# A fused sliding-window attention and SwiGLU kernel: a shorter VectorE chain for one token group, and attention sinks on four row groups of TensorE

## The chip, the cores and the metric

The kernel runs on one core of a Trainium2 chip. The metric is the device time of one execution in microseconds (us). Runs of one kernel mostly agree within 0.3%, but this kernel's runs differ by about 0.6 us with the clock that TensorE was granted; each run records its mean clock, and I compare like with like where it matters. A run more than 1.5% above the fastest of its kernel is marked slow and left out of the ratios (eight runs of run 15 below, one of run 8).

In the profile lines, PE is TensorE's matmuls, PEld its weight loads, DVE VectorE, ACT ScalarE and POOL GpSimd. PSUM is the memory that matmuls write; the kernel holds eight banks of it. A *row group* is 32 of the 128 rows of TensorE's array: `32*128` in a line is a matmul on one of them. *Half clock* is a stretch in which the granted clock reads 0.50.

Ratios below are the mean time of one kernel's fast runs over the mean time of the fast runs of the kernel before in the same rounds, so they are not quite the ratio of the medians that stand beside them. Brackets hold 95% intervals.

## The reference

Four batches, 8 heads, 768 positions, head size 64. Each query sees the last 128 keys and the first four (the *sinks*). The result, 3072 tokens of 512 numbers, goes through a gated feed-forward block.

```python
scores = scale * np.matmul(q, k.transpose(0, 1, 3, 2))
keep = (pos[None, :] < 4) | ((rel >= 0) & (rel < 128))   # rel = query position - key position
a = softmax(np.where(keep, scores, -1e9))
x = np.matmul(a, v)            # then [tokens, heads * 64]
g = x @ w_gate
return (g * sigmoid(g) * (x @ w_val)) @ w_out
```

## The kernel before

The 3072 tokens are cut in 12 attention *groups* of 256 tokens, three for each batch, and in eight feed-forward *token blocks* (three of 256, four of 512, one of 256). A unit of feed-forward work is a gate matmul set `pg`, a value set `pv`, and an element-wise pair `u`, `ht` on VectorE. A `weave` puts attention steps between the `pg` and the `pv` of a unit: transposes `T`, scores `S`, sink scores `K`, value products `PV`, output transposes `X`. Groups that are not the first of their batch have sinks: there `PV` starts with a full-row matmul of the sink probabilities `es` with a block-diagonal tile `vsb` of sink values.

```python
def step_K(g):                             # sink scores
    ps = bank([P, 256], FP32, "pk")
    for p in range(NP2):                   # 4 pairs of heads, 32 PSUM rows each
        nc.tensor.matmul(ps[32 * p:32 * p + KW], kss[:, b, p], qTs[b][:, p, c * 256:(c + 1) * 256], ...)
    es_t[g] = espool.tile([P, 256], BF16, tag="es", name="es")
    nc.scalar.activation(es_t[g], ps, AF.Exp, scale=scale)

def step_PV(g, j, hh):                     # 128 tokens x 4 heads
    po = bank([P, 4, D + 1], FP32, "o")
    mms = []
    if c > 0:
        mms.append((po, es_t[g][:, j * P:(j + 1) * P], vsbs[b][:, 4 * hh:4 * hh + 4]))
    ...                                    # then the window's 8 matmuls
    def dve():
        nc.vector.reciprocal(rcp, po[:, :, D:D + 1])
        nc.vector.tensor_tensor(xns[g, j]..., po[:, :, 0:D], rcp.broadcast_to([P, 4, D]), op=ALU.mult)
    later.append(dve)

def step_X(g, j, evict="v"):               # normalised rows xn -> xT, the input of the block
    if g >= XB:                            # XB = 4: groups 4 to 11 by DMA transpose
        nc.sync.dma_start_transpose(xTs[tb][:, :, off:off + P], xns[g, j])   # (queued)
    else: ...                              # TensorE transposes px, then a copy to xT

# prologue (cut): group 0
st = [rowp.tile([P, H, 2 * D], FP32, tag="rows", name="st") for _ in range(2)]   # k and q, 512-byte rows
...
pair_S(1); pair_T(3)
nc.vector.tensor_scalar(lt8, th8, float(NS), None, op0=ALU.is_lt)
nc.vector.scalar_tensor_tensor(diag_h, th8, 0.0, lt8, op0=ALU.is_ge, op1=ALU.mult)
pair_mask(0); pair_S(2); step_ks(0); pair_mask(1); ...

# groups 1 and 2
us = [g0[0], (alone, 0, 0), g0[1], (alone, 0, 0), g0[2], g1[0], ...]   # alone: a unit without gates
weave(us, slots((1, PVs(1)[:2]), (3, PVs(1)[2:]),
    (4, [A(step_X, 1, 0, "a"), A(step_X, 1, 1, "a")]), ...))

def pair(ga, gb, sh=0):                    # two groups in one 512-token block
    return [((s, s + 2), Ss(ga)), (s + 2, [K(ga)]), ((s + 4, s + 5, s + 6, s + 7), PVs(ga)),
            ((s + 6, s + 8), Ss(gb)), ((s + 8, s + 9), Xs(ga)), (s + 8, [K(gb)]), ...]
```

The softmax here doesn't subtract the row's maximum and nothing guards it: scores larger than these inputs give would overflow.

## Time and profile before

| | kernel before |
|---|---|
| median time | 248.36 us (248.31 to 248.96, 4 runs) |
| span of the profiled run | 246.7 us, TensorE busy 95% |
| first gate matmul (end of the prologue) | 15.60 us |
| first down-projection matmul `pd` | 64.06 us |
| first gate matmul of token block 3 | 83.84 us |
| from there to the end | 162.86 us |

The last four rows are starts of TensorE groups in the timeline. They cut the run in stretches with different limits: the prologue; groups 1 to 4 and blocks 0 to 2; the long steady part. A change is read by how it moves each milestone, not by shares of busy time. Each kernel has one profile, so a milestone has scatter: three kernels with the changed prologue, word for word, reach the first gate matmul at 20.95, 20.81 and 19.99 us (the changed kernel, runs 3 and 7). The prediction shows the lines for group 1 and for the sinks. Two more views of this trace matter later. The first is VectorE in the prologue (start, length, instruction, in brackets the idle time ahead of it and what ended it):

```profile
8.72 0.41 DVE L497 CAST qT<-pt 128x256 bf16<-128x256 f32 x1
9.06 0.16 DVE L531 TENSOR_SCALAR lt<-th 128x8 f32<-128x8 f32 x1
9.25 0.17 DVE L532 SCALAR_TENSOR_TENSOR diag_h<-th,lt 128x8 bf16<-128x8 f32 x1
9.33 0.55 DVE L516 TENSOR_TENSOR e<-e,mask 128x768 bf16<-128x768 bf16 x1
...
10.18 1.50 DVE L516 TENSOR_TENSOR e<-e,mask 128x768 bf16<-128x768 bf16 x3
```

The four masks follow the last cast at once, and nothing waits for a load. The second is the DMA rate in the first 14 us, in 40 slices of 0.35 us:

```profile
GB/s 0 0 0 0 0 95 110 59 285 350 341 344 347 350 341 338 221 195 192 194 189 191 198 178 164 157 153 158 164 190 187 197 192 199 196 196 167 168 155 156
```

From the tenth slice (3.15 us) the input loads run on a plateau near 345 GB/s.

### The profile page before, as it was taken

The numbers are of one execution on the slowest core, as the hardware profiler recorded it, in microseconds if no ns is written. First come the engines' busy times: TensorE is split into PE (matmuls) and PEld (weight loads), VectorE is DVE, ScalarE is ACT, GpSimd is POOL, SyncE is SP. The second block draws the span as 40 slices with busy tenths as digits, with TensorE's granted clock in tenths as the row PEclk, the third lists the DMA queues.
The fourth block names the chain that finished last, engine by engine and source line by source line (L and its number), as shares of the span: only waits on it lengthen the run. The fifth ranks groups of instructions, "written<-read, shape, count | busy, mean of one in ns | idle before, by whom it ended". The sixth has DMA issues, their size and how long they took to land.

```text
span 246.7 us, 5043 instructions
## 1 busy us (share of the span) xinstructions
PE 235.0 (95%) x1981; PEld 136.5 (55%) x2004; DVE 163.7 (66%) x345; ACT 111.7 (45%) x219; POOL 67.8 (27%) x89
## 2 busy tenths in 40 slices
PE   7796999999999999999999999999999999999994
PEld 3485787787645445444445454445454445478443
DVE  5988378876955199992298993198980389887100
ACT  4893347234654473621564721555611662333112
POOL 8955735984680007250053000000000000000000
PEclk9999799999999999999999999999999999999999
DMA  7999999999999449994479302551103200100132
GB/s 187 183 185 196 191 206 195 156 159 141 156 178 216 144 106 89 128 139 110 128 127 156 51 3 85 148 129 25 43 3 120 92 0 3 43 3 0 43 128 85
DMA packets 100390, 27.61 MB, mean 112 GB/s; under 512 B 85392, under 2 KB 97424, under 8 KB 100368
## 3 DMA queue, kind: packets, MB, share of 16 engines
q0 software_dynamic: 68384, 13.64, 67.4%
q1 hardware_dynamic: 30928, 13.15, 22.9%
q10 hardware_dynamic: 1056, 0.52, 0.7%
q8 instruction: 15, 0.25, 0.4%
q14 instruction: 7, 0.06, 0.1%
HBM read 28.34 MB, written 6.29 MB: 140 GB/s over the span
## 4 chain that ended last, share of the span: by engine, by line
PE 84%; DVE 9%; ACT 4%; issue 1%; DVEq 0%
PE pd L416 25%; PE pv L385 24%; PE pg L385 22%; PE o L329 4%; PE s L283 3%; ACT e L290 3%; DVE ht L399 3%; PE pt L235 2%; DVE xn L335 2%; DVE u L398 1%; PE w L473 1%; DVE e L516 1%; PE pt L489 1%; DVE e L295 1%; ACT th L392 0%
## 5 line engine op out<-in xcount | busy, mean ns | idle before, releaser
L385 PE MATMUL pv<-xT,wv 128*128 128x256 bf16 (+1 forms) x374 | 74.7, 328 | 1.5 <-DVE ht L399 0.9
L392 ACT ACTIVATE th<-pg 128x512 f32<-128x512 f32 x72 | 43.5, 605 | 71.3 <-PE pg L385 69.3
L385 PE MATMUL pg<-xT,wg 128*128 128x256 bf16 (+1 forms) x380 | 74.8, 328 | 0.2
L398 DVE SCALAR_TENSOR_TENSOR u<-th,pg 128x512 bf16<-128x512 f32 x72 | 49.2, 683 | 34.4 <-ACT th L392 34.1
L416 PE MATMUL pd<-wo,ht 128*128 128x512 bf16 (+1 forms) x291 | 65.0, 370 | 0.6 <-issue 0.2
L399 DVE TENSOR_TENSOR ht<-u,pv 128x512 bf16<-128x512 bf16 x72 | 49.5, 688 | 11.9 <-PE pv L385 5.4
L385 PEld LDWEIGHTS <-wg 128*128 128x128 bf16 x384 | 37.8, 99 | 25.5 <-issue 0.2
L385 PEld LDWEIGHTS <-wv 128*128 128x128 bf16 x384 | 34.7, 99 | 21.2 <-issue 2.8
L290 ACT ACTIVATE e<-s 128x512 bf16<-128x512 f32 (+1 forms) x88 | 42.9, 583 | 3.1 <-PE s L283 3.0
L416 PEld LDWEIGHTS <-ht 128*128 128x128 bf16 x300 | 28.0, 98 | 28.6 <-issue 0.3
L420 ACT ACTIVATE ot<-pd 128x512 f32<-128x512 f32 (+1 forms) x25 | 14.6, 583 | 50.9 <-PE pd L416 50.9
L295 DVE TENSOR_TENSOR e<-e,mask 128x1024 bf16<-128x1024 bf16 (+1 forms) x44 | 27.0, 649 | 3.3 <-ACT e L290 3.2
L110 POOL DMA_DIRECT2D nat<-in_k_dram x16 | 14.2, 901 | 46.5 <-DMA qT<-nat 42.4
L121 POOL DMA_DIRECT2D va<-in_v_dram x24 | 21.5, 912 | 5.4 <-DMA nat<-in_q_dram 2.6
L335 DVE TENSOR_TENSOR xn<-o,rcp 128x256 bf16<-128x256 f32 x48 | 20.4, 424 | 1.7
L329 PEld LDWEIGHTS <-e 128*128 128x128 bf16 x352 | 16.8, 98 | 7.1 <-DVE e L516 1.0
L329 PE MATMUL o<-va,e 128*128 128x65 bf16 x352 | 18.4, 193 | 0.7 <-DVE e L516 0.7
L110 POOL DMA_DIRECT2D nat<-in_q_dram x16 | 14.3, 909 | 1.8 <-DMA nat<-in_k_dram 1.6
L334 DVE RECIPROCAL rcp<-o 128x4 f32<-128x4 f32 x48 | 8.5, 177 | 7.4 <-PE o L329 7.2
L283 PE MATMUL s<-qT,kT 64*128 64x128 bf16 (+1 forms) x240 | 12.9, 237 | 0.0
L283 PEld LDWEIGHTS <-kT 64*128 64x128 bf16 x240 | 7.7, 94 | 6.9 <-issue 6.4
L329 PE MATMUL o<-vsb,es 128*128 128x260 bf16 x32 | 8.8, 274 | 0.3 <-ACT es L309 0.3
(56 smaller groups left out, 89.9 us busy)
## 6 DMA issues: line engine op xcount, KB each, us to landing
out_dram<-ot SPq DMA_DIRECT2D x23, 256.0 KB
va<-in_v_dram POOLq DMA_DIRECT2D x24, 128.0 KB, 7.5
nat<-in_k_dram POOLq DMA_DIRECT2D x16, 128.0 KB, 6.7
nat<-in_q_dram POOLq DMA_DIRECT2D x16, 128.0 KB, 7.3
wo<-in_moe_w_out_dram POOLq DMA_DIRECT2D x4, 384.0 KB, 12.3
wg<-in_moe_w_gate_dram POOLq DMA_DIRECT2D x4, 256.0 KB, 8.4
wv<-in_moe_w_val_dram POOLq DMA_DIRECT2D x4, 256.0 KB, 8.9
rows<-in_k_dram POOLq DMA_DIRECT2D x6, 128.0 KB, 9.0
```

Of the source, the lines that this page charges most:

```text
L110: nc.gpsimd.dma_start(x[:, i, j].rearrange("p (h d) -> p h d", d=D), src[b, :, t0:t0 + P].rearrange("h p d -> p h d"))
L121: nc.gpsimd.dma_start(va[:, j, :, 0:D], v[b, :, t0:t0 + P].rearrange("h p d -> p h d"))
L283: nc.tensor.matmul(pss[2 * pp + h][:, col:col + n], kTs[b][r, p, kk:kk + P], qTs[b][r, p, qq:qq + n], start=True, stop=True)
L290: nc.scalar.activation(e_t[g][:, h0 + h, lo:512], pss[2 * pp + h][:, lo:512], AF.Exp, scale=scale)
L295: nc.vector.tensor_tensor(e, e, m[:, :, lo:512].broadcast_to([P, 2, 512 - lo]), op=ALU.mult)
L329: nc.tensor.matmul(o, l, r, start=(i == 0), stop=(i == len(mms) - 1), skip_group_check=True)
L335: nc.vector.tensor_tensor(xns[g, j][:, 256 * hh:256 * (hh + 1)].rearrange("p (h d) -> p h d", h=4), po[:, :, 0:D], rcp.broadcast_to([P, 4, ...
L385: nc.tensor.matmul(ps[:, i * n:(i + 1) * n], ws[fi][:, c, fo * P:(fo + 1) * P], x[:, c], start=(c == 0), stop=(c == DMC - 1))
L392: nc.scalar.activation(th, pg, AF.Tanh, scale=0.5)
L398: nc.vector.scalar_tensor_tensor(u, th, 1.0, pg, op0=ALU.add, op1=ALU.mult)
L399: nc.vector.tensor_tensor(hts[tb][:, f:f + two].rearrange("p a n -> p (a n)"), u, pv, op=ALU.mult)
L416: nc.tensor.matmul(po, hts[tb][:, f, ts * P:(ts + 1) * P], wos[f // n][:, f % n, lo:hi], start=(f == 0), stop=(f == DFC - 1))
```

## The change

The intent is fourfold. Half of group 1's division goes from VectorE to ScalarE, and the two units without gates go away. The sinks of a group become four matmuls of 32 rows each, on four row groups of TensorE, into four PSUM banks that are opened together. The sink scores move to the first scores of a group. Group 2's outputs come later and are evicted by ScalarE. For the new rows, the sink values `vcf` are needed twice, so 64 partitions of them are copied to the other 64.

```diff
-    diag_h = const.tile([P, H], BF16)
+    diag_h = const.tile([P, 4], BF16)
-    th8 = const.tile([P, H], FP32)          # lt8 the same
+    th8 = const.tile([P, 4, 4], FP32)
-            nc.sync.dma_start(vcf[32 * p + NS * w:..., :, 0:D], ...)
+        r = 32 * (h // 4) + NS * (h % 4)
+        nc.sync.dma_start(vcf[r:r + NS, :, 0:D], ...)
@@ step_ks, step_vsb
-            nc.vector.tensor_copy(kss ...)   # 2 in all
+            nc.vector.tensor_copy(kss ...)   # 4 in all
-        vsb = const.tile([P, H, D + 1], BF16, tag=f"vsb{b}", name="vsb")
+        vsb = const.tile([P, 4, D + 1], BF16, tag=f"vsb{b}", name="vsb")
@@ step_K: 4 matmuls of 256 columns become 8 of 128, two accumulating on each 32 rows of PSUM
@@ new
+    def step_sinks(g):
+        for j in range(2):
+            for hh in range(2):
+                r = slice(32 * (2 * j + hh), 32 * (2 * j + hh + 1))
+                pos[j, hh] = bank([P, 4, D + 1], FP32, "o")
+                nc.tensor.matmul(pos[j, hh], es_t[g][r], vsbs[b][r], start=True, stop=False, ...)
@@ step_PV
+        if c > 0 and j == hh == 0:
+            step_sinks(g)
+            if norm == "a":
+                for hq in range(4):
+                    nc.scalar.activation(xn[:, hq], po[:, hq, 0:D], AF.Copy, scale=rcp[:, hq])
@@ prologue, between pair_T(3) and pair_mask(0)
+    nc.vector.tensor_reduce(diag_h, lt8..., op=ALU.max)
+    nc.vector.tensor_copy(out=vcf[64:128], in_=vcf[0:64])
@@ schedule
-    us = [g0[0], (alone, 0, 0), g0[1], (alone, 0, 0), g0[2], g1[0], g1[1],
+    us = [g0[0], g0[1], g0[2], g1[0], g1[1],
-        (1, PVs(1)[:2]), (3, PVs(1)[2:]), (4, [X(1, 0), X(1, 1)]), ... (9, [K(2)]), ... (12, Xs(2)),
+        (1, PVs(1)[:2] + [A(step_PV, 1, 0, 1, "a"), A(step_PV, 1, 1, 1, "a"), flush]),
+        (2, [X(1, 0), X(1, 1)]), ... (6, [K(2)]), ... (11, [X(2, 0, "a"), X(2, 1, "a")]),
-        (s + 2, [K(ga)]), ... (s + 8, [K(gb)])      # pair(); the same for group 11
+        (s, [K(ga)]), ... (s + 6, [K(gb)])
```

## The prediction

> **What bounds the kernel now.** I read the page first (busy shares, slices), then the waits of TensorE, then the chain of work that ended last, in order of time, and last the timeline around each place where TensorE stood still.
>
> ```profile
> PE 235.0 (95%) x1981; PEld 136.5 (55%) x2004; DVE 163.7 (66%) x345; ACT 111.7 (45%) x219; POOL 67.8 (27%) x89
> ...
> PEclk9999799999999999999999999999999999999999
> ```
>
> TensorE has work 95% of the time, so only two things can shorten the run: less time in TensorE instructions, or fewer of its gaps. The clock row has one slice (the fifth, 24.7 to 30.8 us) at 7 instead of 9. Its cause is in the chain of waits (start, length, what):
>
> ```profile
> 10.18 1.51 DVE e L516 x3
> ...
> 18.26 0.69 DVE e L295
> 18.95 0.62 DVE u L398
> ...
> 23.92 0.43 DVE xn L335
> ...
> 24.41 0.28 PE px L358 x2
> 24.69 1.14 PE pv L385 x8
> 25.83 1.71 PE pg L385 x8
> 27.54 1.44 PE pv L385 x8
> 28.98 0.87 PE pg L385 x8
> ```
>
> From 18.26 to 24.41 the end is set by VectorE (mask, u, ht, and the four pairs reciprocal + normalisation of group 1, with u and ht of the second gate unit between the pairs). TensorE waits for the last normalised rows. After that wait eight 256-column matmuls take 1.14, 1.71 and 1.44 us where the same eight take 0.87 at the end of the fence. The timeline and the windows of 1 us (engine busy, then granted clock, DMA share, GB/s) show both halves:
>
> ```profile
> 23.86 0.40 PE L358 MATMUL px<-ident,xn 128*128 128x128 bf16 x4 [2.19 <-DVE xn L335]
> ...
> 25.00:26.00 1.00, 1.00 (x8) 0.77 (x6) 0.13 (x1) 0.31 (x1) 1.00 (x2) 0.58 1.95 170
> 26.00:27.00 1.00, 1.00 (x7) 0.70 (x5) 0.56 (x1) 0.00 (x0) 1.00 (x2) 0.50 2.36 166
> 27.00:28.00 1.00, 1.00 (x7) 0.69 (x6) 0.00 (x0) 0.42 (x1) 0.89 (x2) 0.50 1.62 192
> ```
>
> Group 1 thus costs a wait of 2.2 us and then a half clock worth 0.27+0.84+0.57 = 1.7 us: 3.9 us in all. Group 2 has a small copy of it: TensorE waits 0.35 us for its sink scores at 40.95, and 0.38+0.15 us for normalised rows at 46.5 and 47.1. After 50 us the waits of TensorE are three of 0.2 to 0.4 us (value matmuls waiting for ht, i.e. for a PSUM bank).
>
> What a sink costs, in the steady part:
>
> ```profile
> 131.53 0.27 PE L329 MATMUL o<-vsb,es 128*128 128x260 bf16 x1
> ...
> 131.64 0.41 PE L329 MATMUL o<-va,e 128*128 128x65 bf16 x8
> ...
> 131.89 1.03 PE L385 MATMUL pv<-xT,wv 128*128 128x512 bf16 x4
> ...
> 134.06 0.61 PE L283 MATMUL s<-qT,kT 64*128 64x128 bf16 x12
> ...
> 134.61 1.04 PE L385 MATMUL pv<-xT,wv 128*128 128x512 bf16 x4
> ```
>
> Read starts, not lengths: matmuls overlap. The block with a sink takes 131.89-131.53 = 0.36 us; in group 9, which has no sinks, the same eight matmuls take 0.24. So a sink matmul costs TensorE 0.12 us, not its 274 ns, and all 32 cost 3.8 us.
>
> **What the Trainium skill says.** "TensorEngine Tiling (Array Packing)", Key Properties: tiles operate independently, but changing the tiling mode drains TensorE; its Gotcha 1 says different row tiles must write different PSUM banks (hence the four banks). The trace agrees for two row groups: the scores are 2048 columns in 64-row halves; at 0.216 us for 512 columns (four take 0.86) that is 0.86 us one after the other, 0.43 us two at a time, and the fence shows 0.55. They do run in pairs, and entering and leaving the mode costs 0.12. Four row groups no run here has shown yet.
> "TensorE: Matmul & The Clock Gate", Part 1, What's actually happening: the clock falls to half after an idle window of about 3.4 us that runs freely. The trace agrees on the half (0.50) and on about 3 us of it; it also shows that a wait of 2.2 us with little work around it is enough.
> "ScalarE: Activation LUTs", What ACT_TABLE_LOAD costs: an ACTIVATE takes 186 + 0.833 N ns, each per-partition operand adds about 93, and neighbours overlap by about 93. The trace gives 605 ns for N=512 (formula 612); the kernel before has no per-partition operand.
> "VectorE: DVE Perf Modes", The TRN2 errata: fp32 tensor_tensor takes (N+151)/0.96 ns. The trace has vsb at 701 ns for N=520 (formula 699).
>
> **Part by part.**
>
> *Prologue, added work.* VectorE is the chain there: the masks at 10.18 follow one another without a gap. Ahead of the last masks the change puts two more kss copies (0.17 each, by the two at 9.80 to 10.14) = 0.34; a small reduction, about 0.17 (lt and diag take 0.16 and 0.17); the copy of vcf into the upper half, 64x260 fp32, about 0.28 (the shortest 128x256 fp32 cast took 0.28); wider lt and product, 0.03. Sum 0.82 us, all on the path, since the next transposes, scores and exponentials queue behind the last mask (11.68 becomes 12.5). vsb halves from 0.70 to 0.43 (formula above) and moves into a VectorE gap of 0.59 us at 12.8: free. The sink exponential halves its columns: 0.43 to about 0.32, so from there the shift is about 0.7.
>
> *Group 1.* New VectorE order: last mask (ends 18.95+0.72 = 19.67), u, ht (1.41 us as before, 21.08), two reciprocals (21.4), then the two pairs for the first halves (0.55 each: 21.95 and 22.5). The second halves go to ScalarE: eight copies of 128x64 with a per-partition scale, 186+93+53 = 332 ns each, 240 apart after the overlap (an estimate from the ScalarE page), from 21.27 to 23.3. TensorE itself, started at 15.6+0.82, is through the second gate unit, the PVs and the third unit's first half at about 22.0. So it waits again, but in pieces: 0.3 for the first transposes, about 1.0 for the last, and the value matmuls start near 23.45 where they started at 24.69. Then a new wait: th of that unit and the two evictions (0.55 apart, by the 1.13 for two at 24.18) follow the eight copies on ScalarE, so xT is ready at 24.9 while TensorE is free at 24.3. The next gate matmuls start at 24.9 instead of 25.83: 0.93 gained, of which 0.27 is the clock. If the clock stays up, the 0.84+0.57 behind it are gained too: 2.34. The waits sum to 1.8 us in pieces instead of 2.3 in one, and the prologue (gaps of up to half a microsecond, clock 1.00 throughout) shows that pieces do not pull it down. I give 75% that it stays.
>
> *Group 2.* Sink scores one unit earlier: the 0.35 goes. Output one unit later: the 0.53 goes. But ScalarE now evicts in the unit just ahead of the first one that reads it: after that unit's first half, th takes 0.6 and two copies 1.1, so xT is ready at about +1.83 us, while TensorE comes at +1.27 (px 0.39, value 0.87): a new wait of about 0.55. Net 0.35 gained.
>
> *Sinks.* Four at once in 32-row tiles: 0.11 for one 260-column pass plus 0.12 for the two mode changes, 0.25 with a little for weights, against 4x0.12 = 0.48 before. 0.2 for each group: seven groups that are not in group 1's wait give 1.4 us. Sink scores: eight matmuls of 128 columns in two accumulating rounds instead of four of 256, the same columns, but the second round's weights go to columns in use: I take +0.05 for each group, 0.4 lost. Net 1.0.
>
> *Where that is not all real.* In the units with PV, VectorE's cycle (u 0.80, ht 0.60, reciprocal 0.21, normalisation 0.47 from start to start) is 2.08 us and so is TensorE's (131.53 to 133.62): a faster TensorE runs into VectorE, and all four output banks are now taken at the first PV and the last held until the fourth, while the next group's scores want four of the eight banks. I take 0.3 us off: 0.7.
>
> Sum: 2.34+0.35+0.7 = 3.4 us with the clock up, about 2.0 if it still falls. Weighted 3.1; I round up to 3.5, since the sinks of group 2 and shorter ScalarE work can add a few tenths: 244.8 us.
>
> **Rivals.** (a) The clock drop stays, or moves into the prologue, where TensorE waits 0.8 us longer for masks. For it: my 1.8 us of waits is not far from 2.3. Against: the pieces. Time 246 to 247. (b) The four sinks don't overlap, or the mode change costs more than the 0.12 seen. For: no four-row-group pass in this trace. Against: the scores pair perfectly. Sinks then give nothing or lose 0.5: 245.5 to 246. (c) PSUM banks become the bound: value matmuls wait for ht or u at each pair's first scores (now with the sink scores in the same unit). For: those waits of 0.2 to 0.4 exist. Against: the sink scores left the unit where they occur. Costs up to 2 us: 246.5. (d) The gain is larger: the vcf and kss work fits in gaps that I counted as full, ScalarE's copies are shorter, no wait at group 1 or 2 remains. That would be about 1.8+0.55 more: 242.5. (e) The vcf copy waits for its own DMA, whose last issue ends at 6.5 us: up to 1 us, and everything behind it shifts.
>
> **Range and chances.** The spread is the clock (1.4), group 1's remaining wait (1), the sinks (0.8) and the banks (1), mostly independent: about 2.2 us either way, 242.5 to 247.0. A gain over 2% needs 243.34 or less, i.e. rival (d) in good part: 0.25. Slower by 2% would need nearly all rivals at once and more: 0.02.
>
> **What will show it.** The clock row without the 7; no wait of 2 us on px; masks of the prologue ending about 0.8 us later; the eight ScalarE copies 0.24 apart; the four sinks starting within 0.1 us of one another and the block 0.25 us long; new TensorE waits for xT copies ahead of the fourth gate unit and of the third token block. Wrong if the clock still falls, if the sinks start 0.11 apart, or if the waits for ht, u or xn after 50 us exceed 2 us in sum.

## The result, and the profile after

The changed kernel takes 249.78 us (median, 249.5 to 250.4, 4 runs) against 248.36; ratio 1.0055 [1.003, 1.0081]. It is 5.0 us slower than predicted and outside the range.

| us | before | after | moved by |
|---|---|---|---|
| first gate matmul | 15.60 | 20.95 | +5.35 |
| first `pd` | 64.06 | 64.96 | +0.90 |
| token block 3 | 83.84 | 84.62 | +0.78 |
| block 3 to the end | 162.86 | 162.88 | +0.02 |

So the stretch between the prologue and the first `pd`, where groups 1 and 2 lie, did gain: 5.35 - 0.90 = 4.45 us. The prologue, priced at 0.82 us, took it all and more. In the page's clock row the 7 of before is gone, but an 8 stands two slices earlier:

```profile
PEclk9989999999999999999999999999999999999999
```

VectorE in the prologue, as shown of before:

```profile
10.07 0.41 DVE L523 CAST qT<-pt 128x256 bf16<-128x256 f32 x1
10.40 0.38 DVE L557 TENSOR_SCALAR lt<-th 128x16 f32<-128x16 f32 x1
10.81 0.18 DVE L558 SCALAR_TENSOR_TENSOR lt<-th,lt 128x16 f32<-128x16 f32 x1
11.02 0.18 DVE L559 TENSOR_REDUCE diag_h<-lt 128x4 bf16<-128x16 f32 x1
12.59 0.52 DVE L561 COPY vcf<-vcf 64x260 f32<-64x260 f32 x1 [1.39 <-DMA vcf<-in_v_dram]
13.14 0.56 DVE L542 TENSOR_TENSOR e<-e,mask 128x768 bf16<-128x768 bf16 x1
...
14.25 1.50 DVE L542 TENSOR_TENSOR e<-e,mask 128x768 bf16<-128x768 bf16 x3
```

Read it line against line. The last cast is 1.35 us later (10.07 against 8.72). The selector takes until 11.20 us, 0.4 more. The copy of the sink values then waits 1.39 us for its loads, which were issued by 7.3 us and land at 12.32 (the chain of waits has them as one piece of 5.04 us), and takes 0.52 itself. So the first mask starts at 13.14 instead of 9.33. With two more copies of sink keys between, the last mask ends at 15.76 instead of 11.68. What TensorE does with this, in its timeline and in windows of 1 us (length, busy us of PE, PEld, DVE, ACT, POOL; then granted clock, DMA share, GB/s):

```profile
13.76 0.24 PE L346 MATMUL o<-va,e 128*128 128x65 bf16 x2 [1.87 <-DVE e L542]
14.86 0.24 PE L346 MATMUL o<-va,e 128*128 128x65 bf16 x2 [0.86 <-DVE e L542]
...
15.97 1.76 PE L233 MATMUL pt<-ident,rows 64*64 64x64 bf16 x32
17.66 1.06 PE L346 MATMUL o<-va,e 128*128 128x65 bf16 x16
...
16.00:17.00 1.00, 1.00 (x26) 1.00 (x26) 0.97 (x4) 0.09 (x1) 0.91 (x2) 0.59 1.44 189
17.00:18.00 1.00, 1.00 (x21) 0.83 (x18) 0.18 (x1) 0.73 (x2) 0.00 (x0) 0.50 1.46 196
18.00:19.00 1.00, 1.00 (x20) 0.84 (x19) 0.65 (x3) 0.35 (x1) 0.61 (x1) 0.50 1.44 194
```

Behind waits of 1.87, 0.86, 0.23 and 0.23 us, 3.19 in sum, the clock is halved. That these waits are the trigger is not shown: runs 1 and 3 take most of them away, and the clock is halved all the same. In the chain of waits the transposes take 1.69 us (1.01 before), the value products 1.00 (0.59) and the scores 0.58 (0.37): 1.30 us. The slow clock that the change removed at group 1 now sits in the prologue. 4.08 us on the last mask and 1.30 us of clock make 5.38, which is the shift of the first gate matmul to 0.03 us.

Group 1 after (compare the fence of 18.26 to 28.98 us in the prediction):

```profile
23.67 0.29 PE L326 MATMUL o<-vsb,es 32*128 32x260 bf16 x4
23.89 1.15 PE L346 MATMUL o<-va,e 128*128 128x65 bf16 x32
...
27.54 0.23 PE L384 MATMUL px<-ident,xn 128*128 128x128 bf16 x1 [0.18 <-ACT xn L357]
27.61 1.04 PE L411 MATMUL pv<-xT,wv 128*128 128x256 bf16 x8
28.99 1.03 PE L411 MATMUL pg<-xT,wg 128*128 128x256 bf16 x8 [0.34 <-ACT xT L387]
```

The wait of 2.2 us has become 0.18 + 0.34, and 256-column matmuls keep 0.87 us for eight from start to start. From the first gate matmul to the second gate set after group 1 the kernel needs 3.43 us less: 1.98 up to the first gate set (the shorter wait, and some 0.2 of clock in the value set ahead of it), 1.45 by the clock behind it. Group 2 gains about another 1.0.

### The profile page after: what moved, and what is told of

It reads as the page before. It is cut to its first block, busy times and chain, and to the rows that moved or that the text cites. A ratio compares the mean times of both kernels' runs of the same rounds, so it can differ in the third digit from the quotient of the medians.

```text
span 247.5 us, 5122 instructions
## 1 busy us (share of the span) xinstructions
PE 234.6 (95%) x2012; PEld 134.4 (54%) x2036; DVE 162.3 (66%) x351; ACT 113.0 (46%) x229; POOL 67.8 (27%) x89
## 3 DMA queue, kind: packets, MB, share of 16 engines
q10 hardware_dynamic: 1056, 0.52, 0.8%
## 4 chain that ended last, share of the span: by engine, by line
PE 83%; DVE 6%; DMA 4%; ACT 4%; issue 1%; ACTq 0%; DVEq 0%
PE pd L442 25%; PE pv L411 23%; PE pg L411 23%; PE o L346 4%; PE s L285 4%; DMA st<-in_q_dram 2%; PE pt L233 2%; DMA vcf<-in_v_dram 2%; ACT e L292 2%; DVE ht L425 1%; DVE u L424 1%; DVE e L542 1%; ACT xT L387 1%; DVE e L297 1%; ACT xn L357 1%
## 5 line engine op out<-in xcount | busy, mean ns | idle before, releaser
L411 PE MATMUL pg<-xT,wg 128*128 128x256 bf16 (+1 forms) x378 | 73.3, 325 | 1.1 <-ACT xT L387 0.7
L411 PE MATMUL pv<-xT,wv 128*128 128x256 bf16 (+1 forms) x375 | 73.4, 325 | 0.8 <-DVE xn L360 0.2
L411 PEld LDWEIGHTS <-wv 128*128 128x128 bf16 x384 | 34.0, 98 | 20.4 <-issue 1.9
L346 PEld LDWEIGHTS <-e 128*128 128x128 bf16 x352 | 16.0, 99 | 12.0 <-DVE e L542 3.7
L360 DVE TENSOR_TENSOR xn<-o,rcp 128x256 bf16<-128x256 f32 x46 | 19.5, 424 | 1.6
L285 PE MATMUL s<-qT,kT 64*128 64x128 bf16 (+1 forms) x240 | 13.6, 243 | 0.4 <-DVE ht L425 0.4
L233 PE MATMUL pt<-ident,rows 64*64 64x64 bf16 x192 | 7.5, 256 | 0.0
```

What stands on the lines that cost most here:

```text
L285: nc.tensor.matmul(pss[2 * pp + h][:, col:col + n], kTs[b][r, p, kk:kk + P], qTs[b][r, p, qq:qq + n], start=True, stop=True)
L346: nc.tensor.matmul(o, l, r, start=(c == 0 and i == 0), stop=(i == len(mms) - 1), skip_group_check=True)
L360: nc.vector.tensor_tensor(xn, po[:, :, 0:D], rcp.broadcast_to([P, 4, D]), op=ALU.mult)
L411: nc.tensor.matmul(ps[:, i * n:(i + 1) * n], ws[fi][:, c, fo * P:(fo + 1) * P], x[:, c], start=(c == 0), stop=(c == DMC - 1))
```

## The experiments

After the result I held that the prologue had eaten the gain ("theory A" in the texts on record), with the copy's wait as its core. The rival that became "theory D" after the first batch is a floor from the transfers at token block 3. Letters are explained in the texts where they are used. All runs gave correct results.

**1. The copy later.** In the changed kernel the copy goes from ahead of the first mask to just ahead of the tile that needs it.

```diff
-    nc.vector.tensor_copy(out=vcf[64:128], in_=vcf[0:64])      # before pair_mask(0)
     flush()
+    nc.vector.tensor_copy(out=vcf[64:128], in_=vcf[0:64])
     step_vsb(0)
```

> The changed kernel with the one copy of vcf into its upper half moved from ahead of the first mask to just ahead of vsb of batch 0, three masks and two normalisations later. Theory A (the copy, which waits 1.39 us for the last of its eight loads and then takes 0.52 us, stands in front of the four masks; the idle TensorE behind it brings a half clock worth 1.3 us): 1.4+0.55+1.3 = about 3.2 us less than the changed kernel's 249.8, so 246.6 us, ratio to before 0.993; masks end near 13.8 us instead of 15.8 and the clock stays at 1.00 from 15 to 20 us. Theory B (the copy costs its own 1.9 us, the half clock comes anyway because all loads land a us later in this kernel): 247.9. Theory C (the loss is in the new schedule of groups 1 and 2 or in the sinks, not in the prologue): no change, 249.8.

Measured: 252.57 us (251.47 to 253.67), ratio 1.0153 [1.0125, 1.0181]. The first gate matmul did come 1.91 us earlier (19.04), and the kernel got slower. Milestones: first `pd` 63.08 (1.9 earlier), but block 3 at 86.08, 1.5 *later*: there TensorE waits 3.18 us for the transposed outputs of group 4, and runs at half clock behind the wait. So the time was gone from the prologue, and the end came later all the same: theory A alone misses. It misses on the clock too, which it expected at 1.00 from 15 to 20 us: the prologue's waits are down to 0.69 + 0.23 + 0.23 us, and the windows still read

```profile
15.00:16.00 1.00, 1.00 (x22) 0.83 (x17) 0.86 (x2) 0.58 (x1) 0.62 (x2) 0.50 1.59 202
```

**2. The copy alone, on the kernel before.** A copy of the same size ahead of the first mask, into a scratch tile.

```diff
+    vcx = const.tile([64, B, D + 1], FP32)
+    nc.vector.tensor_copy(out=vcx, in_=vcf[0:64])
     pair_mask(0)
```

> The kernel before with one added copy of vcf (64x260, into a scratch tile that nobody reads) ahead of the first mask; nothing else changes and the result is right. Theory A: the masks wait for the load of vcf, 2 us or more later than 9.33 us, the half clock comes too, and the chain of group 1 passes it on: 250.5 to 252.5 us, ratio 1.01 to 1.017. Theory C: only the copy's 0.5 us, 248.9 us.

Measured: 249.95 us, ratio 1.005 [1.0034, 1.0066], between the two forecasts. The copy took 0.29 us and waited for nothing, since in the old layout it reads half of the loads only. The first gate matmul moved from 15.60 to 17.10. This test is not clean: the scratch tile also moved the tiles after it, which runs 14 and 17 show to matter.

**3. Filler against the slow clock.** Eight matmuls of zeros ahead of the prologue's value products, in the changed kernel.

```diff
     pair_mask(3)
+    fill(8, bank([P, 512], FP32, "w"))
     step_PV(0, 0, 0)
```

> The changed kernel with eight matmuls of zeros (8 x 0.216 = 1.7 us at full clock) on TensorE in its gap ahead of the first PV of group 0; masks and copy stay where they are. If the half clock from 16 to 19.5 us comes of that gap and costs what the chain shows (transposes 1.69 against 1.01, PV 1.00 against 0.59, scores 0.58 against 0.37): about 1.2 us less than the changed kernel, 248.5 us, and the windows show 1.00. If the half clock is not from the gap or costs nothing: 249.8.

Measured: 250.77 us, ratio 1.0082 [1.0059, 1.0105], above both forecasts. The filler ran up to 13.5 us, right ahead of the first value products at 13.59: it filled the wait of 1.87 us and left those of 0.90, 0.23 and 0.23 behind it. The transposes still take 1.76 us, as in the changed kernel's timeline, at half clock:

```profile
17.00:18.00 1.00, 1.00 (x21) 0.83 (x18) 0.04 (x1) 0.73 (x2) 0.17 (x1) 0.50 1.46 197
```

So the longest wait alone is not what halves the clock. What does stays open. The record shows only that all five profiles with the changed prologue (one with the copy moved) have this half clock, and none of the nine with a short prologue has it.

**4. A short prologue.** The selector is built at 3 us when VectorE is idle; the sink keys after the first flush; the copy and the sink values after group 1's sink scores.

```diff
+    (iota of th8 first; selector's three instructions after mask0's set-up)
-    step_ks(0)                       # between the masks
     flush()
+    step_ks(0)
     ...
     step_K(1)
+    nc.vector.tensor_copy(out=vcf[64:128], in_=vcf[0:64])
+    step_vsb(0)
     step_S(1, 1)
```

> The changed kernel with all four additions to the prologue out of the way of the masks: the head selector built in VectorE's idle time at 3.2 us, the sink keys after the first two normalisations, the copy and vsb of batch 0 after the sink scores of group 1 are issued. Theory A: the masks end as early as before or 0.9 us earlier (11 to 11.7 us by the load of the inputs), and group 1, group 2 and the sinks give what they gave: 1.9 (group 1, chain) + 1.45 (clock) + 1.1 (rest) = 4.5 us less than before, 244 us, ratio 0.982 (0.978 to 0.988). Theory C: 249 to 250.

Measured: 252.03 us, ratio 1.0127 [1.0104, 1.0151], where theory A forecast 244, although the first gate matmul is back at 15.55. The lines of block 3:

```profile
77.76 2.10 PE L446 MATMUL pd<-wo,ht 128*128 128x512 bf16 x8
84.37 1.11 PE L415 MATMUL pg<-xT,wg 128*128 128x512 bf16 x4 [4.50 <-DMA xT<-xn]
...
86.71 1.89 PE L415 MATMUL pv<-xT,wv 128*128 128x512 bf16 x4
```

Whatever is gained earlier, block 3 does not start before 84.4 us here, because the transposed outputs of group 4 have not landed; and the wait brings the half clock (1.89 us for four matmuls that take 1.03 otherwise). The kernel before starts this block at 83.84 and shows no such wait: it sits near the floor. The floor is not one fixed time: where a profile shows this wait, it ends at 83.43 (run 12), 84.37 (this run), 84.95 (run 15) or 86.08 us (run 1).

**5 to 8. The floor taken away.** One number sends group 4's outputs through TensorE instead of the DMA transpose. It was tried on the short prologue, on the changed kernel, and on the kernel before, with the kernel before once more as a control.

```diff
-    XB = 4
+    XB = 5
```

> The kernel before, unchanged, as a control for one thing: in its first profile the last input for the casts lands at 6.25 us, in the changed kernel and in three of its variants at 6.8 to 7.5 us. If that is chance, this profile can show 6.8 to 7.5 too, with the first gate matmul 0.5 to 1.2 us later than 15.6 us and a time within 0.4% of 248.4; if it belongs to the changed program, 6.25 again.

> The short prologue of b1, with the outputs of group 4 transposed by TensorE (as for groups 0 to 3) and not by the DMA queue; one constant changed from 4 to 5. Theory D (the DMA engines are full until about 80 us; the transposed outputs of group 4, on which the fourth token block waits, land at 84 us or later however early TensorE is, so every microsecond won earlier is lost again there, with a half clock on top): the wait of 4.5 us and the half clock of about 1.7 us go, the fourth block starts near 80.3 us, and the time is 252.0-4.5-1.7 = about 246, at best 244.5 us (ratio 0.982 to 0.992). Rival E (something else in the new schedule takes over, such as the next transposed inputs or PSUM banks): the fourth block starts early but the time stays above 249.

> The changed kernel with group 4's outputs transposed by TensorE. Theory D: in its profile TensorE reached the fourth block at 84.62 us without a wait, so it was late enough; the change adds 8 transposes (0.4 us) and removes at most a small wait in some runs: 249.3 to 250.2 us. If the changed kernel is already held by that landing: 2 us less, 247.8.

> The kernel before with group 4's outputs transposed by TensorE. Theory D: the kernel before reaches the fourth block at 83.84 us, just at the landing; 0.4 us of transposes added, a wait of at most a few tenths removed: 248.2 to 249.0 us. If it is well below 248 the kernel before was held by the landing too.

| | median us | ratio | first gate | block 3 |
|---|---|---|---|---|
| before again | 248.91 | 0.9981 [0.9958, 1.0004] | 15.62 | 83.85 |
| short prologue, XB = 5 | 245.61 (245.38 to 245.97) | 0.9843 [0.9807, 0.9879] | 16.02 | 80.56 |
| changed, XB = 5 | 250.04 | 1.0039 [1.0022, 1.0055] | 19.99 | 84.14 |
| before, XB = 5 | 248.95 | 1.000 [0.9978, 1.0022] | 15.72 | 82.74 |

The control's cast starts at 6.23 us, as in the first profile (6.25). The three others came out as theory D forecast. The floor is shown: the same switch is worth 6.4 us (252.03 to 245.61, in two rounds) where TensorE arrives early, and nothing where it arrives late. All runs of the second row have a full clock, and their spread is narrow. The second row, called the *short kernel* below, is the base of the next runs.

**9. The old sinks on the short kernel.** Full-row sink matmuls, old layouts, old slots for the sink scores: the sink part of the change, reversed.

```diff
-        if c > 0 and j == hh == 0:
-            step_sinks(g)
+            mms.append((po, es_t[g][:, j * P:(j + 1) * P], vsbs[b][:, 4 * hh:4 * hh + 4]))
     (step_K, step_ks, step_vsb, th8, lt8, diag_h, vcf's rows as before; no copy of vcf)
```

> The best kernel so far (short prologue, group 4's outputs transposed by TensorE: 245.61 us, ratio 0.9843), with the sinks as before: full-row sink matmuls, sink keys, selector and sink scores in the old layout and slots. Everything else (group 1 and 2's shorter chain) stays. Theory of the traces (after token block 3 the sink part gains nothing, since both kernels take 163 us from there to the end): 245.4 to 246.1 us, ratio within 0.002 of the best, and block 3 to the end again 163.0 us. Rival, the prediction's (the sink part saves 0.25 to 0.7 us in all): 245.9 to 246.3. Second rival (full-row sinks would be cheaper, since four banks are held from the first PV on): below 245.2. The prologue can also gain some tenths, since four copies of the sink keys and the copy of the sink values become two and none.

Measured: 245.60 us (245.54 to 245.70), ratio 0.986 [0.9832, 0.9888]: as good as with the new sinks (245.61). One part of that is the tiles' addresses, which went back as well (run 14). Against run 14, which has these addresses and the new sinks, the old sinks are 0.58 us slower (the two ran on different chips; by their ratios, 0.986 and 0.9834, it is 0.65, and the intervals of the ratios overlap). The milestones say where: block 3 at 80.70 against 79.91, and from there to the end 163.1 against 163.0. The new sinks gain before block 3 and next to nothing after it.

**10. Each sink just ahead of its own value products.**

```diff
-        if c > 0 and j == hh == 0:
-            step_sinks(g)
-        po = pos.pop((j, hh)) if c > 0 else bank(...)
+        po = bank([P, 4, D + 1], FP32, "o")
+        if c > 0:
+            nc.tensor.matmul(po, es_t[g][r], vsbs[b][r], start=True, stop=False, ...)
```

> The best kernel so far, with each row-group sink matmul issued just before its own PV instead of four in a row, so that an output bank is opened only when its PV runs. If holding four banks from the first PV costs something (waits of the next scores for banks, 0.22 and 0.18 us per unit in the trace of the change), 244.8 to 245.3 us, and the unit that also holds next scores falls from 3.1 us back towards 2.7. If the four in a row are what makes the sinks cheap (0.22 us for four, by overlap in four row groups), each sink costs about 0.1 to 0.12 us: seven groups in blocks 3 to 7, four sinks each, 28 x 0.06 = 1.7 us slower at most, 246.0 to 247.2. If both cancel, 245.4 to 245.9.

Measured: 251.00 us (250.67 to 251.42), ratio 1.0077 [1.0048, 1.0106], 5.4 us slower than the short kernel and far above what I expected (the expectation also counts seven groups with sinks from block 3 on; there are five). The timelines of block 4 give the price of a sink. First the old full-row form (run 9), one unit from `pg` to `pg`:

```profile
127.64 1.03 PE L396 MATMUL pg<-xT,wg 128*128 128x512 bf16 x4
128.50 0.28 PE L331 MATMUL o<-vsb,es 128*128 128x260 bf16 x1
...
129.72 1.03 PE L396 MATMUL pg<-xT,wg 128*128 128x512 bf16 x4
```

Then the four row groups at once (short kernel), a unit with the sinks and one without:

```profile
125.73 1.03 PE L415 MATMUL pg<-xT,wg 128*128 128x512 bf16 x4
126.69 0.29 PE L330 MATMUL o<-vsb,es 32*128 32x260 bf16 x4
126.91 0.42 PE L350 MATMUL o<-va,e 128*128 128x65 bf16 x8
...
128.03 0.81 PE L415 MATMUL pg<-xT,wg 128*128 128x512 bf16 x3
...
130.00 1.03 PE L415 MATMUL pg<-xT,wg 128*128 128x512 bf16 x4
```

And one row-group sink for each value product (run 10):

```profile
130.00 1.03 PE L417 MATMUL pg<-xT,wg 128*128 128x512 bf16 x4
130.96 0.28 PE L341 MATMUL o<-vsb,es 32*128 32x260 bf16 x1
131.17 0.42 PE L352 MATMUL o<-va,e 128*128 128x65 bf16 x8
...
132.29 1.03 PE L417 MATMUL pg<-xT,wg 128*128 128x512 bf16 x4
```

Units take 2.08, 2.30 with and 1.97 without sinks, and 2.29 us. So a full-row sink costs 0.11 us; four row-group sinks together cost 0.33; one alone costs 0.32. The price is in entering and leaving the mode (from `pg` to the sink 0.96 us instead of 0.86, from the sink to the next matmul 0.21 or 0.22 instead of 0.11), and it is paid once for four. The new form thus saves 4 x 0.11 - 0.33 = 0.11 us for each group in this part, not 0.23.

Where that went after block 3 shows in a few units. In the short kernel the units at 93.27, 130.00 and 139.22 us, where the next group's scores or the next sinks want banks, hold waits: they take 3.51, 3.14 and 2.57 us where their matmuls need 2.51, 2.85 and 2.30. In run 10, which opens banks one at a time, such waits are gone: its units with next scores take 2.83 and 3.17, exactly 2.29 + 0.54 and 2.29 + 0.65 + 0.23 for their scores and sink scores. From block 3 on there are five groups with sinks. At 4 x 0.32 - 0.33 = 0.95 they make 4.75 us more for the mode changes, less 1.00 + 0.29 + 0.27 = 1.56 of waits: 3.19. From block 3 to the end, run 10 takes 166.2 us and the short kernel 163.0.

**11. Groups 1 and 2 on their old schedule, on the short kernel.** 

```diff
-    us = [g0[0], g0[1], g0[2], g1[0], g1[1],
+    us = [g0[0], (alone, 0, 0), g0[1], (alone, 0, 0), g0[2], g1[0], g1[1],
     (the slots of before for groups 1 to 4; sink scores keep the new place)
```

> The best kernel so far, with groups 1 and 2 on the schedule of before: two units without gates for group 1's outputs, VectorE divides all of them, group 2's outputs two units later in the same order as before. Theory (the part of the change at groups 1 and 2 is where the gain is, 3.4 + 1.0 us in the traces of before and changed kernel, 1.45 of it clock): 248.0 to 249.3 us, ratio to before 0.994 to 1.001, token block 3 reached 3 to 3.5 us later than the best's 80.56. Rival (the gain of the best kernel comes from the full clock of its runs and the TensorE transposes, not from group 1): 245.6 to 247.0.

Measured: 247.26 us (246.84 to 249.26, 22 runs), ratio 0.9948 [0.9929, 0.9967], between the two forecasts. The runs fall in two sorts. Fourteen with a clock of 0.997 to 1.0 took 246.84 to 247.60; eight with 0.992 or 0.993 took 248.5 to 249.3. So the shorter chain is worth about 1.4 us at full clock, and it also spares the half clock, which costs another 1.9 us in some of the runs (medians 246.96 and 248.81; the profiled run, at 248.60, has a 7 in the fifth slice of its clock row again).

**12. Addresses alone, on the kernel before.** I had seen that the input casts start later in every program whose constant tiles differ in size from before's.

```diff
-    one = const.tile([P, 1], FP32)
+    onex = const.tile([P, 1 + 260], FP32, name="one")
+    one = onex[:, 0:1]
```

> The kernel before with one constant tile made 1040 bytes a partition larger, which moves the addresses of all tiles after it and adds no instruction. All programs with the old addresses cast their last q input's first half at 6.25 us, all others (the changed kernel's and the one with a scratch tile) at 6.9 to 7.5. If addresses cause this, the cast of the second half starts at 6.9 to 7.5 us here and the kernel is 0.5 to 1.0 us slower than before; if the other instructions do, it stays at 6.25 and the time is before's, ratio 0.998 to 1.002.

Measured: 248.51 us (248.21 to 251.22), ratio 1.000 [0.9973, 1.0026]. The cast in question starts at 6.88 instead of 6.25 and the first gate matmul at 16.52 instead of 15.60, which looks like the address theory; the total does not move, perhaps because the floor at block 3 is near (this profile shows a wait of 0.17 us for the transposes there). But built again, this kernel has its first input tile at byte 68864, 1024 further and again a multiple of 256, and its loads keep the rate of the kernel before (compare run 17):

```profile
GB/s 0 0 0 0 0 80 75 92 262 350 339 345 347 348 333 330 242 199 195 194 189 197 190 187 162 160 151 157 161 187 193 196 189 202 195 195 175 166 159 153
```

So its late cast has another cause, which stays open, and the time at which one profile's cast starts is no clean test of addresses.

**13. The second scores later, on the short kernel.**

```diff
-                ((s + 6, s + 8), Ss(gb)), ... (s + 6, [K(gb)]),
+                ((s + 8, s + 10), Ss(gb)), ... (s + 8, [K(gb)]),
```

> The best kernel so far (245.61 us), with the second group's scores and sink scores of a pair two units later (units 8 and 10 in place of 6 and 8), so that fewer banks of four open outputs and four scores are wanted at once. If the held banks are what gives the sink part's gain back (the units at 93.3, 130.0 and 139.2 us of the best kernel take 3.51, 3.14 and 2.57 us, against 2.51, 2.85 and 2.30 from their matmuls alone, sum 1.56 us), 244.0 to 244.9 us, and those waits are gone. Rival: they are the price of VectorE and ScalarE being busy there, the waits move to the units of the second group's outputs, 245.3 to 246.3.

Measured: 245.25 us (245.21 to 245.33), ratio 0.9842 [0.981, 0.9874], between the two forecasts. Both theories were partly right. Block 3's gates fell from 26.01 to 25.01 us, its waits gone. Blocks 4 and 5 lost 0.45 and 0.47: one unit there now needs twelve scores in the same unit as the next sinks (3.97 us). The next run puts the sink scores alone back to the slots of before.

```diff
-                (s, [K(ga)]), ... (s + 6, [K(gb)])          # K(2), K(4), K(11) likewise
+                (s + 2, [K(ga)]), ... (s + 8, [K(gb)])
```

> The best kernel so far, with the sink scores back at the slots of before (with the second scores of a group). The move only shifts 0.23 us of matmuls from one unit to another, so 245.4 to 245.8, ratio within 0.001 of the best; if the early sink-score bank is what makes the unit at 130.0 us wait (3.14 against 2.85), 0.3 to 0.6 us faster, 245.0 to 245.3.

Measured: 245.86 us, ratio 0.9867 [0.9835, 0.99], slightly worse than 245.61. The unit of 3.14 us becomes 2.68 and the one of 2.38 becomes 2.98. Moving the sink scores earlier is worth 0.25 us at most; the runs of the two kernels overlap (245.68 to 246.16 and 245.38 to 245.97).

**14. The old addresses with the new sinks.** The short kernel, with the sink values' tile at its old size (half unused) and the selector's number tiles in bf16, so that all later tiles are where they were in the kernel before.

```diff
-        vsb = const.tile([P, 4, D + 1], BF16, tag=f"vsb{b}", name="vsb")
+        vsb8 = const.tile([P, 8, D + 1], BF16, tag=f"vsb{b}", name="vsb")
+        vsb = vsb8[:, 0:4]
-    th8 = const.tile([P, 4, 4], FP32)       # lt8 the same
+    th8 = const.tile([P, 4, 4], BF16)
```

> The best kernel so far with the constant tiles padded so that all tiles have the size and address of the kernel before (the sink values' tile keeps its old size, the selector's number tiles become bf16). Four programs with these addresses cast the first half of the last q input at 6.23 to 6.36 us, with old or new rows for the sink values never separated; ten others at 6.82 to 7.46. If addresses decide, 6.2 to 6.4 here, and the first gate matmul 0.4 to 1.0 us earlier than 16.02; time 245.0 to 245.5. If the new rows of the sink values' loads decide, 6.8 to 7.5 and 245.5 to 245.8.

Measured: 245.02 us (244.94 to 245.31), ratio 0.9834 [0.9802, 0.9866]. The cast starts at 6.12 and the first gate matmul at 14.87, 1.15 us earlier. The rows of the sink values' loads are the new ones here, so addresses decide, not rows. The first gate matmul bears it out over more profiles: 15.55 to 16.30 us in the six short-prologue kernels with the changed kernel's addresses (runs 4, 6, 10, 11 and 13's two), 14.87 to 15.06 in the three with the old ones (runs 9, 14 and 16).

**15. Groups 1 and 2's new schedule alone, on the kernel before.** Prologue, sinks and transposes as before; only the units and slots, and the division by ScalarE, are the changed kernel's.

```diff
-    us = [g0[0], (alone, 0, 0), g0[1], (alone, 0, 0), g0[2], g1[0], g1[1],
+    us = [g0[0], g0[1], g0[2], g1[0], g1[1],
-        (1, PVs(1)[:2]), (3, PVs(1)[2:]), ...
+        (1, PVs(1)[:2] + [A(step_PV, 1, 0, 1, "a"), A(step_PV, 1, 1, 1, "a"), flush]), ...
```

> The kernel before with only groups 1 and 2 on the new schedule (two units without gates gone, half of group 1's division on ScalarE, group 2's outputs later and evicted by ScalarE); prologue and sinks as before, group 4's outputs by DMA transpose. Theory (the DMA floor at token block 3): block 3 would be reached at 80.3 to 81 us by the matmuls' sum, but the transposed outputs of group 4 land at 84 or later, so a wait of 2.5 to 4.5 us there, a slow clock behind it, and 249 to 252 us. Rival, the prediction's (what is gained at groups 1 and 2 is kept): 246.0 to 247.5.

Measured: 251.83 us (247.69 to 252.51, 14 runs). Two of the runs have a full clock and took 247.69 and 247.85; the twelve others have 0.986 to 0.993 and took 249.4 to 252.5 (eight of the twelve are marked slow; the ratio from the six fast runs is 1.0016 [0.9972, 1.006], no difference). The two at full clock are some 0.6 us below the kernel before at full clock (248.20 to 248.86 in this round). The profile, of a run of 250.93 us, shows at block 3 where the gain goes:

```profile
77.67 3.19 PE L424 MATMUL pd<-wo,ht 128*128 128x512 bf16 x13
84.95 1.15 PE L393 MATMUL pg<-xT,wg 128*128 128x512 bf16 x4 [4.09 <-DMA xT<-xn]
```

The part of the change that I was surest of gives by itself no gain that fast runs show, and in most runs a loss.

**16. The best of all.** Run 14 with the second scores later in block 3 alone.

```diff
+    def pair(ga, gb, sh=0, w=(6, 8)): ... ((s + w[0], s + w[1]), Ss(gb)) ...
-        *pair(5, 6),
+        *pair(5, 6, w=(8, 10)),
```

> The kernel with the old addresses (245.02 us), with the second scores of token block 3 alone at units 8 and 10. In the run that moved them in all blocks, block 3's gates took 25.01 us against 26.01, block 4's 26.92 against 26.47 and block 5's 25.46 against 24.99. So block 3 alone should give 1.0 us: 243.8 to 244.3 us, ratio to before 0.979 to 0.981. Rival: what is gained at block 3 is lost at a later wait (transposed outputs or inputs by DMA arriving as late as before), 244.7 to 245.1.

Measured: 244.13 us (244.07 to 244.20), ratio 0.9803 [0.9777, 0.9828]. It beats both kernels, the one before by 4.9 us by the medians of the round; whether that is 2% the interval leaves open. The unit in block 3 before and after this edit (short kernel first) falls from 3.51 to 1.97 us; 0.54 of that are its scores, which only moved to a later unit:

```profile
93.27 1.03 PE L415 MATMUL pg<-xT,wg 128*128 128x512 bf16 x4
...
95.35 0.32 PE L289 MATMUL s<-qT,kT 64*128 64x256 bf16 x3 [0.43 <-DVE ht L429]
95.91 1.04 PE L415 MATMUL pv<-xT,wv 128*128 128x512 bf16 x4 [0.23 <-DVE xn L364]
```

```profile
92.63 1.03 PE L416 MATMUL pg<-xT,wg 128*128 128x512 bf16 x4
93.50 0.41 PE L351 MATMUL o<-va,e 128*128 128x65 bf16 x8
93.74 1.02 PE L416 MATMUL pv<-xT,wv 128*128 128x512 bf16 x4
```

**17. The changed kernel with the old addresses.** The edit of run 14 on the changed kernel, nothing else.

> The changed kernel (249.78 us), with the constant tiles padded so that all tiles have the addresses of the kernel before, nothing else. If addresses cost the changed kernel its late casts, the first half of the last q input is cast at 6.1 to 6.4 us (7.28 in the changed kernel), the first gate matmul comes at 19.6 to 20.2 (20.95), and the time is 248.4 to 249.4 if the rest follows; the wait for the copy of the sink values, which hangs on its own loads, keeps the first gate at 20.5 to 21 and the time at 249.5 to 250 if those loads do not land earlier too.

Measured: 248.38 us (247.98 to 249.08, 22 runs), ratio 0.9976 [0.9965, 0.9988], where the changed kernel has 1.0055. The first gate matmul comes at 19.72 instead of 20.95, the last q input's cast at 6.15 instead of 7.28, and the DMA rate of the first 14 us changes with it. First the changed kernel, then this one:

```profile
GB/s 0 0 0 0 0 64 66 38 306 348 338 347 315 294 287 291 279 211 192 195 189 196 193 189 182 164 157 152 158 169 185 195 192 190 202 195 194 169 165 157
```

```profile
GB/s 0 0 0 0 0 104 114 75 310 348 342 341 350 347 341 326 213 195 189 192 195 190 189 176 164 158 154 160 168 187 191 193 193 199 195 198 161 171 153 157
```

From the thirteenth to the seventeenth slice the changed kernel moves 279 to 315 GB/s, where this one (and the kernel before, above) moves 326 to 350 in four slices and is through one slice earlier. The build puts the first input tile at byte 67840 of each partition in the kernel before, a multiple of 256, and at 65856 in the changed one, 64 bytes past such a multiple. The difference, 1984 bytes, is the smaller `vsb` (four times 1056 - 544 bytes, tiles being rounded up to 32) less 64 for the selector. The inputs arrive in rows of 512 bytes. The Trainium skill, "DMA: Bandwidth & Descriptors", section "How a descriptor splits into AXI transactions", says that a descriptor is cut at multiples of 256 bytes and that one which starts off them pays for an extra piece. By its rule, which it words for reads, I estimate two transactions and 16 beats of 32 bytes for an aligned row of 512, three and 18 for one shifted by 64 bytes.

The traces agree as far as they go. In the fourteenth and fifteenth slice the nine programs with an aligned first input (before and its control, before with XB = 5, runs 9, 12, 14, 15, 16 and 17) move 333 to 350 GB/s, the eleven others, which are 32 or 64 bytes off, 281 to 307. The 1024 packets of the q input take 27.0 to 27.4 ns in the mean in the nine, 29.8 to 30.2 in the eleven. The cast follows less strictly: 6.12 to 6.36 us in eight of the nine and 6.82 to 7.47 in the eleven, but 6.88 in run 12. That it is the count of transactions, and not something else that goes with the address, no run shows.

## Why the prediction was wrong

**The step that failed is the prologue, "Sum 0.82 us, all on the path".** It measured 5.35 us. Its own terms were near: sink keys 0.34 (measured 0.27 between the masks), the reduction 0.17 (0.18). The copy took 0.52 instead of 0.28, and the wider selector 0.2 instead of 0.03 (in run 7, with the same prologue, 0.29 and nothing). What was missing is larger than the sum:

- the copy's wait for its loads, 1.39 us. It stands in the prediction as rival (e), "up to 1 us, and everything behind it shifts", and then enters neither the sum nor the range. Run 1 shows that the copy and its wait were worth 1.91 us at the first gate matmul.
- inputs that land 1.35 us late by the last cast. The prediction did not see that smaller constant tiles move the addresses of the input tiles. Run 17 gives 1.23 us at the first gate matmul, of which part can be scatter (run 7 has 19.99 without it), and 0.6 to 0.8% of the time (medians 249.78 and 248.38, ratios 1.0055 and 0.9976).
- 1.30 us of half clock in the prologue, rival (a) in its second form ("moves into the prologue"). I had argued with waits 0.8 us longer; they came to 3.19 against 0.66 before, 2.5 longer. The clock itself stays unexplained (runs 1 and 3).

**Group 1 was right in mechanism and low in size.** Predicted 0.93 + 1.41 = 2.34, measured 1.98 + 1.45 = 3.43 between milestones. The eight ScalarE copies ran 0.20 us apart (0.24 estimated) at 329 ns each (332), and the new wait for the evictions is 0.34 us (0.6 estimated, 24.9 - 24.3). **Group 2**: net 0.35 predicted, about 1.0 measured; the new wait of 0.55 came as 0.5 us at 50.72.

**But a gain there is not a gain at the end,** which no rival named. The floor at block 3 would have taken most of it even with a short prologue: runs 4 and 15 lose 4.50 and 4.09 us to it, and the half clock behind that wait makes them, in most runs, slower than before. The prediction followed TensorE's waits of the kernel before, where this one does not exist because TensorE arrives at 83.84 us. With the floor gone (short kernel) the groups' schedule is worth 1.4 us, and some 3.2 us with the half clock it avoids (run 11). The prediction put the half clock's worth at 1.41 us as if every run had it: in the last round the kernel before had a clock of 0.998 or more in 10 of 27 runs (248.19 to 248.72 us) and 0.992 or 0.993 in 15 (248.90 to 249.23), only some 0.6 us apart; the other two, at 0.985, took 250.44 and 250.52.

**The sinks:** predicted 0.7 in all; measured 0.58 at equal addresses (run 9 against run 14). The size of the whole was right, its parts were not: four row groups cost 0.33 us, not 0.25, and from block 3 on almost nothing is left (163.1 and 163.0 us). The waits of rival (c) came: 1.56 us in three units, under its "up to 2 us". Runs 10, 13 and 16 are consistent with held banks as their cause. They change the bank order and VectorE's order at once, though, so held banks and VectorE's turn aren't separated.

**The checks of the last paragraph:** the clock row lost its 7, but has an 8 instead; the wait on `px` is gone; the masks end 4.1 us later, not 0.8; the copies are 0.20 apart and the four sinks start together, as said (0.22 us to the next matmul; the whole cost of 0.33 has 0.10 ahead of them); the waits that the timeline lists after 50 us stay below 2 us in sum. Two slips in the working change nothing: the pieces of group 1's wait add up to 1.9 us, not 1.8, and 2% below 248.36 is 243.4. The range had four terms, all from groups 1 and later; the prologue had none, and it was off by 4.5 us.

## What to carry to other kernels

Before adding an instruction to a chain that sets the end, ask of each operand when it lands; a copy of 0.3 us whose load lands late costs the landing, and the clock behind it can fall as well (1.30 us here, though what halved it is open). Before counting a gain, look for the next transfer downstream that only just arrives in time: it has no wait in the old profile and takes the gain in the new one. When constant tiles change size, keep the tiles that loads write to at their old alignment (multiples of 256 bytes went with the faster rate in all 20 profiles here), and compare the DMA rates of the two traces before explaining anything else.

## What the Trainium skill lacked or had wrong

- "DMA: Bandwidth & Descriptors": it explains the cut at 256 bytes, but gives no rate for shifted rows in SBUF. Here 512-byte rows that start 32 or 64 bytes off ran at 281 to 307 GB/s in two slices where aligned ones ran at 333 to 350, without overlap in 20 profiles; in the cleanest pair the cast that waits for them started 1.13 us later (7.28 against 6.15).
- The same page, section "Latency and other measured facts", gives 2 us as the HBM access latency under high load, but has no figure from issue to landing for small loads behind large ones. Here eight loads of 4 KB, issued by 7.3 us behind the weights' loads, landed at 12.32: 5.0 us.
- "TensorEngine Tiling (Array Packing)": it says that a change of mode drains TensorE, without a figure. Here one 32-row matmul of 260 columns among full-row ones cost 0.32 us, four in four row groups 0.33, one full-row matmul of the same columns 0.11.
- "TensorE: Matmul & The Clock Gate": its rule is an idle window of about 3.4 us. Here the clock was halved after waits of 1.87 and 0.86 us with 0.24 us of work between them, and in run 17 within 1.5 us of the last matmul (the matmuls end at 10.52, the clock reads 1.00 to 11.75 and 0.50 from 12.00). That it differs between runs of one kernel (run 15: full clock in 2 of 14) goes with the free-running window of that page.
